# Windowed attention and a low-rank mixer on one core: load order, shared Q/K buffers and new places for three batches' attention

## The chip, the core and the metric

The kernel runs on one core of one Trainium2 chip. The core has five engines that run side by side, each through its own list of instructions in order: TensorE (PE, matrix products; PEld are its weight loads), VectorE (DVE), ScalarE (ACT), GpSimd (POOL) and SyncE (SP). POOL and SP here also issue the DMAs that bring data from HBM to the on-chip memory SBUF and back. Matrix products land in a small accumulator memory, PSUM, from which DVE and ACT read. An instruction waits on semaphores that other engines and DMAs count up.

The metric is the device time of one execution in microseconds; several runs of the kernel are made, and their median is given.

## What is computed

Inputs are q, k and v of shape (8 batches, 8 heads, 576 positions, 64), the low-rank factors U (576 x 32) and V (32 x 576), and two weight matrices w_ch1 (512 x 2048) and w_ch2 (2048 x 512). In short form:

```python
scores = (q @ k.transpose(0, 1, 3, 2)) / 8          # per batch and head
scores = where(0 <= row - column < 64, scores, -1e9)  # a causal window of 64
attn = softmax(scores) ; a = attn @ v
x = a.transpose(0, 2, 1, 3).reshape(8, 576, 512)
h = x.transpose(0, 2, 1) @ U @ V                     # mixes positions, rank 32
u = x + h.transpose(0, 2, 1)
out = u + maximum(u @ w_ch1, 0) @ w_ch2              # per position
```

Results are float32; the kernel works in bfloat16 with float32 accumulation.

## The kernel before

The 8 x 576 = 4608 positions are also 9 chunks of 512. The two big products over w_ch1 and w_ch2 run chunk by chunk (function `mlp`, L635 to L680): 16 pieces `ch1`, each four matmuls of 512 columns and a relu on ACT or DVE, and 16 pieces `ch2` of four matmuls each, whose every fourth adds u on DVE (`osb`) and sends 128 rows out through SP. These 32 pieces, and an empty one behind them, are the slots 0 to 32 of a chunk.

The attention of a batch is cut into small pieces (function `attention`, L238 to L629), and each piece is hung behind a slot of the chunk before the one that needs it. Batch 0 is worked off at the start, batch c + 1 within chunk c. The tables `PLACE`, `PLACE_0`, `PLACE_1` and `PLACE_2` (L683 to L711) give the slot for each piece: T or TX turns K and Q, S multiplies them and takes the exponential on ACT, M multiplies with the window mask on DVE, PV multiplies with V and divides by the row sums on DVE, U and V are the two low-rank products, and UT turns the result u into the layout that `ch1` reads. Nothing reorders this: `tc.manual_schedule()` keeps each engine's instructions in the order in which the program emits them. The frame around it adds the waits: an instruction that reads a buffer waits for the last one that wrote it in program order, and one that writes waits for earlier readers.

Batches 0 and 1 are loaded in a grouped layout, 96 partitions with 6 positions each (tiles `kg` and `qg` of a pool of four, L104 to L121), and turned on PE into `kf` and `qf` (pieces `TK` and `TQ`, L270 to L280); ACT copies K out of PSUM, and DVE copies Q. From batch 2 on K and Q arrive in a natural layout, 128 positions at a time, in `kn` and `qn` (two buffers each, L91), and SP turns them by DMA (`TX`, L282 on). There is one `kf` and one `qf`. V arrives in `vA`; a copy shifted by 64 positions, `vB`, is made by `shift_v` (L146 to L152): on POOL for batches 0 and 1, on DVE from batch 2 on.

POOL issues all loads in this order: K and Q of batch 0, V of batch 0, the two halves of w_ch1 (`w1b`), copies for batch 0's `vB`, K and Q of batch 1, V of batch 1, four quarters of w_ch2 (`w2b`, L225), copies for batch 1's `vB`, then at the head of each chunk's emission (L783 to L796) K and Q of batch 2 (chunk 0 only), V of batch c + 2, and K and Q of batch c + 3. The pieces of chunk c are emitted after these loads, in the loop that fills the slots (L811 on).

PSUM has eight banks: `ps_big` holds two double ones (scores, PV results, the low-rank products), `ps_tp` one (turned tiles), and from chunk 0 on `mm` has three for `ch1` and `ch2`. Batches 0 to 2 turn u on PE with an ACT copy behind (`UT`, L589 to L602); from batch 3 (`NXU = 3`) SP does it by DMA.

At the start the mask is built on POOL and DVE (`maskA`, ones and zeros; `maskB`, zeros and -30000, which PE adds to batch 0's scores), and PE runs idle products (`turn_over`, L716) between pieces.

The softmax here doesn't subtract the row's maximum and nothing guards it: scores larger than these inputs give would overflow.

## Time and profile before

| | |
|---|---|
| median of 3 runs | 322.46 us (321.39 to 322.79) |
| the profiled execution's own time | 320.92 us |
| its span, first to last instruction | 319.2 us |
| PE busy | 304.6 us |
| DVE, ACT, POOL busy | 163.1, 101.8, 103.2 us |
| data moved by DMA | 39.56 MB |
| mean granted PE clock | 0.999 |

The profile is one execution, taken by the hardware. Its times count from the first instruction. "Busy" is the time in which an engine works on something of its own; issuing and waiting are not in it, except that POOL's DMA issues, for which it writes descriptors, are. The list of groups gives for each source line, engine and operation the tiles (output<-inputs), the shape, the count, the busy time and the mean of one in nanoseconds, and then the engine's idle time just before them with what ended most of it. The list of waits says who waited for whom: total in us, times, longest. The order in time gives start, length, engine, line and operation, equal neighbours merged. A matmul of 512 columns is listed with some 380 ns, but neighbours overlap: 64 of them in a row take 13.81 us, so 0.216 us each, and a slot of four 0.86 us.

Chunk 0 begins at 23.69 us, its `ch2` pieces at 43.20, chunk 1 at 64.51, chunk 2 at 98.31 and chunk 3 at 131.66 us. From there on a chunk with attention takes some 32.1 us and one without 27.6.

### The profile page before, as it was taken

Reading aid. Unit: us, or ns where it says so; the run is one execution under the profiler, and the core shown is the slowest. Engines: PE = TensorE matmul, PEld = TensorE weight load, DVE = VectorE, ACT = ScalarE, POOL = GpSimd, SP = SyncE. Lnnn points to the kernel's source line nnn. Section 1 sums busy time; section 2 is a strip of 40 time slices with the busy share of each in tenths; the row PEclk is TensorE's granted clock in tenths of the full one; section 3 lists DMA queues with packets and bytes.
Section 4 is the critical chain, followed back from the end, with each engine's and each line's share of the span. In section 5 each row is a group of like instructions: output and inputs, shape, how many; then the busy total and the mean of one; then the engine's idle time right before and its main releaser. Section 6 shows DMA issues by size and latency. Waiting matters only on the chain.

```text
span 319.2 us, 6811 instructions
## 1 busy us (share of the span) xinstructions
PE 304.6 (95%) x2829; PEld 148.9 (47%) x2855; DVE 163.1 (51%) x293; ACT 101.8 (32%) x160; POOL 103.2 (32%) x134
## 2 busy tenths in 40 slices
PE   6879988999999999899999999999999999999995
PEld 6544543544454544354445444544454444444442
DVE  4464584537675854475647454756474443016011
ACT  2645550337124440345033502350245003201500
POOL 8591696645744744555543400000000000000000
PEclk9999999999999999999999999999999999999999
DMA  7999999999999999999999994444200520020011
GB/s 103 165 225 202 153 201 171 114 185 179 148 124 218 157 127 138 193 179 156 146 204 167 138 162 150 68 100 103 98 2 2 115 100 2 11 87 33 2 66 66
DMA packets 151871, 39.56 MB, mean 124 GB/s; under 512 B 140960, under 2 KB 146080, under 8 KB 151840
## 3 DMA queue, kind: packets, MB, share of 16 engines
q0 software_dynamic: 100096, 18.36, 82.2%
q1 hardware_dynamic: 51744, 20.77, 37.0%
q8 instruction: 22, 0.36, 0.5%
q14 instruction: 9, 0.07, 0.1%
HBM read 37.14 MB, written 9.44 MB: 146 GB/s over the span
## 4 chain that ended last, share of the span: by engine, by line
PE 80%; DMA 13%; POOL 5%; issue 1%; DVE 0%; POOLq 0%
PE psU L665 36%; PE psA L643 35%; DMA qg<-in_q_dram 5%; DMA vA<-in_v_dram 3%; DMA uTc<-un 3%; PE psv L566 2%; DMA qn<-in_q_dram 2%; PE sc L326 2%; PE xw L388 2%; POOL vB L149 1%; POOL vB L152 1%; PE xr L388 1%; PE pshh L487 1%; PE tpu L598 1%; POOL kg L117 1%
## 5 line engine op out<-in xcount | busy, mean ns | idle before, releaser
L665 PE MATMUL psU<-w2b,c 128*128 128x512 bf16 x555 | 130.3, 379 | 3.6 <-DMA w2b<-in_moe_w_ch_dram 2.3
L643 PE MATMUL psA<-uTc,w1b 128*128 128x512 bf16 x576 | 131.0, 380 | 1.6 <-DMA uTc<-un 1.1
L665 PEld LDWEIGHTS <-c 128*128 128x128 bf16 x576 | 55.2, 98 | 66.8 <-issue 3.0
L643 PEld LDWEIGHTS <-w1b 128*128 128x128 bf16 x576 | 54.0, 98 | 66.3 <-DMA uTc<-un 1.6
L654 ACT ACTIVATE c<-psA 128x512 bf16<-128x512 f32 x83 | 49.6, 597 | 91.3 <-PE psA L643 91.2
L674 DVE TENSOR_TENSOR osb<-psU,un 128x512 f32<-128x512 f32 x36 | 24.9, 691 | 82.9 <-PE psU L665 82.7
L652 DVE TENSOR_SCALAR c<-psA 128x512 bf16<-128x512 f32 x61 | 42.1, 690 | 25.8 <-PE psA L643 25.8
L579 DVE TENSOR_TENSOR un<-psv,xs 128x512 bf16<-128x512 f32 (+1 forms) x40 | 25.4, 683 | 22.1 <-PE psv L566 22.0
L135 POOL DMA_DIRECT2D vA<-in_v_dram x32 | 28.1, 888 | 19.8 <-DMA kn<-in_k_dram 6.4
L126 POOL DMA_DIRECT2D qn<-in_q_dram x30 | 25.3, 843 | 22.9 <-DMA vA<-in_v_dram 12.8
L346 ACT ACTIVATE pts<-sc 128x1024 bf16<-128x1024 f32 x32 | 31.4, 1028 | 2.3 <-PE sc L326 2.2
L126 POOL DMA_DIRECT2D kn<-in_k_dram x30 | 25.8, 859 | 15.9 <-DMA vA<-in_v_dram 9.4
L379 ACT ACTIVATE ptl<-low 128x256 bf16<-128x256 f32 x5 | 1.9, 384 | 65.8 <-PE high L326 65.8
L352 DVE TENSOR_TENSOR pts<-pts,maskA 128x1024 bf16<-128x1024 bf16 x28 | 19.1, 682 | 0.1
L326 PEld LDWEIGHTS <-kf 64*64 64x64 bf16 x704 | 9.9, 107 | 8.2 <-issue 8.0
L326 PE MATMUL sc<-qf,kf 64*64 64x128 bf16 (+1 forms) x624 | 12.1, 212 | 1.2 <-issue 0.4
L388 PEld LDWEIGHTS <-pts 128*64 128x64 bf16 x512 | 10.2, 110 | 6.1 <-issue 3.7
L566 PE MATMUL psv<-hh,vrep 128*128 128x512 bf16 x40 | 12.5, 379 | 0.0
L455 DVE TENSOR_TENSOR xs<-xw,rcw 128x896 bf16<-128x896 f32 x10 | 10.9, 1092 | 0.3
L411 DVE TENSOR_TENSOR xs<-xr,rcp 128x512 bf16<-128x512 f32 (+1 forms) x15 | 10.4, 690 | 0.5
L502 ACT CAST hh<-pshh 128x512 bf16<-128x512 f32 x7 | 4.1, 581 | 16.9 <-PE pshh L495 16.9
L601 ACT COPY uTc<-tpu 128x512 bf16<-128x512 bf16 x9 | 5.3, 586 | 11.2 <-PE tpu L598 11.2
(102 smaller groups left out, 159.7 us busy)
## 6 DMA issues: line engine op xcount, KB each, us to landing
out_dram<-osb SPq DMA_DIRECT2D x36, 256.0 KB, 2.4
vA<-in_v_dram POOLq DMA_DIRECT2D x32, 128.0 KB, 10.9
kn<-in_k_dram POOLq DMA_DIRECT2D x24, 128.0 KB, 12.5
qn<-in_q_dram POOLq DMA_DIRECT2D x24, 128.0 KB, 12.1
w1b<-in_moe_w_ch_dram POOLq DMA_DIRECT2D x2, 1024.0 KB, 16.3
w2b<-in_moe_w_ch_dram POOLq DMA_DIRECT2D x4, 512.0 KB, 12.8
kg<-in_k_dram POOLq DMA_DIRECT2D x2, 288.0 KB, 5.8
qg<-in_q_dram POOLq DMA_DIRECT2D x2, 288.0 KB, 6.6
```

The costliest lines, as they stand in the source:

```text
L126: nc.gpsimd.dma_start(out=dst[0:rows, t, :, :], in_=src[b, :, t * P : t * P + rows, :].rearrange("h p d -> p h d"),)
L135: nc.gpsimd.dma_start(out=va[:, t, :, 0:D], in_=v[b, :, t * P : (t + 1) * P, :].rearrange("h p d -> p h d"),)
L326: nc.tensor.matmul(sc[g][r0 : r0 + W, col * W : (col + n) * W], keys_of(j, u, rs), queries_of(j, blk, n, rs), start=not spare, stop=last o ...
L346: nc.scalar.activation(out=dst, in_=sc[:], func=ACT.Exp, scale=scale)
L352: nc.vector.tensor_tensor(out=dst, in0=dst, in1=maskA.rearrange("p g n w -> p g (n w)"), op=ALU.mult)
L388: nc.tensor.matmul(dst, pts[:, h // 2, h % 2, blk, :] if blk < NB - 1 else ptl[:, h // 2, h % 2, :], rhs, start=True, stop=True,)
L579: nc.vector.tensor_tensor(out=u_tiles[g][rs, :], in0=ps[0][rs, n, :], in1=x[rs, t, :, :].rearrange("p h d -> p (h d)"), op=ALU.add,)
L643: nc.tensor.matmul(ps[:], w1b[:, dc, i * P : (i + 1) * P], uTc[:, :, dc, :], start=(dc == 0), stop=(dc == NDC - 1),)
L652: nc.vector.tensor_relu(out=c1[i][:], in_=ps[:])
L654: nc.scalar.activation(out=c1[i][:], in_=ps[:], func=ACT.Relu)
L665: nc.tensor.matmul(acc[t][:], c1[i][:, t * P : (t + 1) * P], w2b[:, i, :], start=(i == 0), stop=(i == NFC - 1),)
L674: nc.vector.tensor_tensor(out=osb[:], in0=acc[t][:], in1=u_tiles[g][:], op=ALU.add)
```

## The change

Seven things change together.

1. **Load order.** The four quarters of w_ch2 are issued before V of batch 1.
2. **Shifted V.** For batch 0 two of the seven copies move from POOL to ACT. Batch 1's copies move from POOL to DVE, as pieces `SV` in slots 21 to 24 of chunk 0, ahead of the PV pieces that read them.
3. **Q/K buffers.** The pool of four grouped tiles goes. Two buffers each, `kr` and `qr`, hold K and Q of batches b and b + 2 in turn: the grouped layout in their first 96 partitions for batches 0 and 1, the natural one from batch 2 on. The calls that issue loads stand where they stood. `kf` and `qf` are doubled.
4. **Places.** The pieces of batches 1 to 3 move: `PLACE_1` and `PLACE_2` change, `PLACE_3` is new, and a place of 100 + s means slot s of the next chunk. Batch 3 turns u on PE (`NXT = 4`).
5. **Mask.** The repeated columns of `maskB` are copied by ACT and DVE; those of `maskA` are made by DVE after batch 0's last piece.
6. **First slots.** In chunk 0 the first two `ch1` pieces run interleaved; which engine takes which relu changes in chunks 0 to 2.
7. **Small ones.** Batch 0's fourth Q copy goes from ACT to DVE, and one more idle product follows the third mask product.

```diff
     NXU = 3
+    NXT = 4
     GP = S // GR
...
     vB = [const.tile([P, NFULL, H, VW], BF16, name=f"vB{i}") for i in range(2)]
-    kn = [const.tile([P, NT, H, D], BF16, name=f"kn{i}") for i in range(2)]
-    qn = [const.tile([P, NT, H, D], BF16, name=f"qn{i}") for i in range(2)]
-    kf = const.tile([P, NT * HP * P], BF16, name="kf")
-    qf = const.tile([P, NT * HP * P], BF16, name="qf")
-    kt, qt = ([f[:, j * S : (j + 1) * S] for j in range(HP)] for f in (kf, qf))
-    kx, qx = (f.rearrange("p (t j w) -> p t j w", t=NT, j=HP) for f in (kf, qf))
+    kr = [const.tile([P, H * GR * D], BF16, name=f"kr{i}") for i in range(2)]
+    qr = [const.tile([P, H * GR * D], BF16, name=f"qr{i}") for i in range(2)]
+    kn, qn = (
+        [r[:, 0 : NT * DM].rearrange("p (t h d) -> p t h d", t=NT, h=H) for r in rs] for rs in (kr, qr)
+    )
+    kfs = [const.tile([P, NT * HP * P], BF16, name=f"kf{i}") for i in range(2)]
+    qfs = [const.tile([P, NT * HP * P], BF16, name=f"qf{i}") for i in range(2)]
     pts = const.tile([P, HP, 2, NB - 1, W], BF16, name="pts")
...
         if grouped:
-            kb = kg_pool.tile([GP, H, GR, D], BF16, name="kg")
-            qb = kg_pool.tile([GP, H, GR, D], BF16, name="qg")
+            kb, qb = (
+                r[0:GP, :].rearrange("p (h c d) -> p h c d", h=H, c=GR) for r in (kr[b % 2], qr[b % 2])
+            )
         else:
...
         if grouped:
-            step = 4 if split else H
-            for h0 in range(0, H, step):
-                hs = slice(h0, h0 + step)
+            for h0, h1 in ((0, 4), (4, 8)) if split else ((0, H),):
+                hs = slice(h0, h1)
                 for t, src in ((kb, k), (qb, q)):
...
             copy(out=vb[0:W, lo:last, :, :], in_=va[0:W, lo + 1 : last + 1, :, :])
+    def shift_high(b, copy, t):
+        copy(out=vB[b % 2][W:P, t, :, :], in_=vA[b % 2][W:P, t, :, :])
+    def shift_low(b, copy, t):
+        copy(out=vB[b % 2][0:W, t, :, :], in_=vA[b % 2][0:W, t + 1, :, :])
...
     for i in range(2):
-        nc.vector.memset(kn[i][W:P, NFULL, :, :], 0.0)
-        nc.vector.memset(qn[i][W:P, NFULL, :, :], 0.0)
+        nc.vector.memset(kn[i][GP:P, NFULL, :, :], 0.0)
+        nc.vector.memset(qn[i][GP:P, NFULL, :, :], 0.0)
...
         nc.gpsimd.dma_start(out=w1b[:, :, lo:hi], in_=w1v[:, :, lo:hi])
-    for t in range(NFULL):
-        shift_v(0, nc.gpsimd.tensor_copy, range(t, t + 1))
+    for t in range(2):
+        shift_high(0, nc.gpsimd.tensor_copy, t)
+        shift_low(0, nc.gpsimd.tensor_copy, t)
+    shift_low(0, nc.gpsimd.tensor_copy, 2)
     for _ in load_kq(1, False):
         pass
-    load_v(1)
     w2v = moe_w_ch2.rearrange("(i p) m -> p i m", p=P)
...
         nc.gpsimd.dma_start(out=w2b[:, i : i + 4, :], in_=w2v[:, i : i + 4, :])
-    for t in range(NFULL):
-        shift_v(1, nc.gpsimd.tensor_copy, range(t, t + 1))
+    load_v(1)
...
         pcs = {}
+        kf, qf = kfs[odd], qfs[odd]
+        kt, qt = ([f[:, j * S : (j + 1) * S] for j in range(HP)] for f in (kf, qf))
+        kx, qx = (f.rearrange("p (t j w) -> p t j w", t=NT, j=HP) for f in (kf, qf))
...
             def f():
-                copy = nc.scalar.copy if spare and j == 3 else nc.vector.tensor_copy
-                copy(out=place_of(qt, j), in_=tr(qb, j, b == 1))
+                nc.vector.tensor_copy(out=place_of(qt, j), in_=tr(qb, j, b == 1))
             return f
...
                 dst = uT_of(g // TPC)[:, g % TPC, :, :]
-                if b >= NXU:
+                if b >= NXT:
                     nc.sync.dma_start_transpose(out=dst, in_=u_tiles[g][:])
...
-    DVE_RELU = {0: (8, 10, 11, 13, 15), 1: (2, 4, 6, 9, 10, 12, 13)}
+    DVE_RELU = {0: (7, 9, 11, 15), 1: (2, 4, 6, 8, 10, 12, 15), 2: (1, 3, 6, 7, 9, 10)}
     DVE_RELU_N = (0, 1, 2, 4, 5, 6, 8)
...
-        def ch1(i):
-            def f():
-                ps = psum["mm"].tile([P, CH], FP32, name="psA", tag="mm")
+        def ch1(*ids):
+            def f():
+                ps = {i: psum["mm"].tile([P, CH], FP32, name="psA", tag="mm") for i in ids}
                 for dc in range(NDC):
-                    nc.tensor.matmul(
-                        ps[:],
-                        w1b[:, dc, i * P : (i + 1) * P],
-                        uTc[:, :, dc, :],
-                        start=(dc == 0),
-                        stop=(dc == NDC - 1),
-                    )
-                c1[i] = c1_pool.tile([P, CH], BF16, name=f"c1_{i}")
-                if i in DVE_RELU.get(c, DVE_RELU_N):
-                    nc.vector.tensor_relu(out=c1[i][:], in_=ps[:])
-                else:
-                    nc.scalar.activation(out=c1[i][:], in_=ps[:], func=ACT.Relu)
+                    for i in ids:
+                        nc.tensor.matmul(
+                            ps[i][:],
+                            w1b[:, dc, i * P : (i + 1) * P],
+                            uTc[:, :, dc, :],
+                            start=(dc == 0),
+                            stop=(dc == NDC - 1),
+                        )
+                for i in ids:
+                    c1[i] = c1_pool.tile([P, CH], BF16, name=f"c1_{i}")
+                    if i in DVE_RELU.get(c, DVE_RELU_N):
+                        nc.vector.tensor_relu(out=c1[i][:], in_=ps[i][:])
+                    else:
+                        nc.scalar.activation(out=c1[i][:], in_=ps[i][:], func=ACT.Relu)
             return f
...
-        return [ch1(i) for i in range(NFC)] + [ch2(t, r) for t in range(TPC) for r in range(4)]
+        ups = [ch1(i) for i in range(NFC)]
+        if c == 0:
+            ups[0:2] = [ch1(0, 1), lambda: None]
+        return ups + [ch2(t, r) for t in range(TPC) for r in range(4)]
...
     PLACE_1 = {
-        "T": [11, 11, 12, 12, 13, 13, 14, 14],
-        "S": [12, 13, 14, 15, 15],
-        "M": [13, 14, 15, 16, 16],
-        "PV": [17, 17, 18, 19, 20],
-        "U": [22],
-        "V": [23, 24, 25],
-        "UT": [25, 26, 27, 28, 29],
-        "TX": [20, 22, 24, 26, 28],
+        "T": [10, 10, 11, 11, 12, 12, 13, 13],
+        "S": [11, 12, 13, 14, 15],
+        "M": [12, 13, 14, 15, 16],
+        "SV": [21, 22, 23, 24],
+        "PV": [21, 22, 23, 24, 24],
+        "U": [26],
+        "V": [27, 28, 28],
+        "UT": [29, 30, 31, 31, 102],
+        "TX": [27, 28, 29, 30, 31],
     }
     PLACE_2 = {
-        "S": [8, 8, 11, 11, 13],
-        "M": [9, 10, 12, 13, 14],
-        "PV": [16, 16, 18, 18, 20],
-        "TX": [13, 14, 15, 16, 17],
-        "U": [21],
-        "V": [23, 24, 25],
-        "UT": [25, 26, 27, 28, 29],
+        "S": [14, 14, 17, 17, 18],
+        "M": [15, 16, 18, 19, 19],
+        "PV": [20, 20, 22, 22, 24],
+        "TX": [20, 21, 22, 23, 24],
+        "U": [26],
+        "V": [27, 28, 29],
+        "UT": [29, 30, 31, 102],
+    }
+    PLACE_3 = {
+        "S": [5, 5, 5, 8, 8],
+        "M": [5, 6, 7, 9, 10],
+        "PV": [12],
+        "TX": [12, 13, 14, 15, 16],
+        "U": [18],
+        "V": [20, 21, 22],
+        "UT": [22, 23, 24, 25, 102],
     }
...
     )
-    pair = maskA[:, 0, 1:3, :].rearrange("p (o n) w -> p o (n w)", o=1)
-    nc.vector.tensor_copy(
-        out=maskA[:, 0, 3:7, :].rearrange("p (o n) w -> p o (n w)", o=2),
-        in_=pair.to_broadcast([P, 2, 2 * W]),
-    )
-    nc.vector.tensor_copy(out=maskA[:, 0, 7, :], in_=maskA[:, 0, 1, :])
     nc.vector.tensor_scalar(
-        out=maskB[:],
-        in0=maskA[:, 0, :, :],
+        out=maskB[:, 0:3, :],
+        in0=maskA[:, 0, 0:3, :],
         scalar1=30000.0,
...
     )
+    def repeat(copy, mask):
+        pair = mask[:, 1:3, :].rearrange("p (o n) w -> p o (n w)", o=1)
+        copy(
+            out=mask[:, 3:7, :].rearrange("p (o n) w -> p o (n w)", o=2),
+            in_=pair.to_broadcast([P, 2, 2 * W]),
+        )
+        nc.vector.tensor_copy(out=mask[:, 7, :], in_=mask[:, 1, :])
+    repeat(nc.scalar.copy, maskB)
     order = "K0 K1 B0 B1 Q0 Q1 S0 S1 K2 K3 B2 Q2 B3 Q3 S2 S3 B4 S4"
...
             load_low_rank()
-        turn_over({"B1": 1, "Q1": 1, "S1": 1, "Q3": 1}.get(what, 0))
-    nc.vector.tensor_copy(out=maskA[:, 1, :, :], in_=maskA[:, 0, :, :])
+        turn_over({"B1": 1, "Q1": 1, "S1": 1, "B2": 1, "Q3": 1}.get(what, 0))
     nc.scalar.copy(out=ub[0][:], in_=uf[0][:])
+    for t in range(2, NFULL):
+        shift_high(0, nc.scalar.copy, t)
     nc.scalar.copy(out=vrep[:, W : W + S], in_=vf[:])
...
         f()
+    repeat(nc.vector.tensor_copy, maskA[:, 0])
+    nc.vector.tensor_copy(out=maskA[:, 1, :, :], in_=maskA[:, 0, :, :])
     first.close()
...
+    all_slots = [[[] for _ in range(NSLOT + 1)] for _ in range(NCH)]
     for c in range(NCH):
-        slots = [[] for _ in range(NSLOT + 1)]
+        slots = all_slots[c]
...
                 for f, s in zip(att[b][part], where[part]):
-                    slots[s].append(f)
+                    all_slots[c + s // 100][s % 100].append(f)
...
                     pass
-            where = {1: PLACE_1, 2: PLACE_2}.get(b, PLACE)
+            where = {1: PLACE_1, 2: PLACE_2, 3: PLACE_3}.get(b, PLACE)
             if b < NXB:
...
                     )
+            if b == 1:
+                def land(t):
+                    def f():
+                        shift_high(1, nc.vector.tensor_copy, t)
+                        if t > 0:
+                            shift_low(1, nc.vector.tensor_copy, t - 1)
+                    return f
+                att[1]["SV"] = [land(t) for t in range(NFULL)]
+                place(b, ("SV",), where)
             place(b, ("S", "M", "PV"), where)
```

More of the change, by code (lines that the diff above doesn't have):

```diff
@@ L59 @@
     const = ctx.enter_context(tc.tile_pool(name="const", bufs=1))
-    kg_pool = ctx.enter_context(tc.tile_pool(name="kg", bufs=4))
     uT_pool = ctx.enter_context(tc.tile_pool(name="uT", bufs=3))
```

## The prediction

> **What bounds the kernel now.** I read the page's engine line and the chain that ended last, then the list of waits of PE, then the order of POOL and PE in time between 28 and 52 us.
>
> ```profile
> PE 304.6 (95%) x2829; PEld 148.9 (47%) x2855; DVE 163.1 (51%) x293; ACT 101.8 (32%) x160; POOL 103.2 (32%) x134
> ```
>
> ```profile
> PE psU L665 <- DMA w2b<-in_moe_w_ch_dram: 2.3, 3, 1.1
> ...
> PE psA L643 <- DMA uTc<-un: 1.1, 1, 1.1
> ```
>
> The span is 319.2 us, and PE is busy for 304.6 of it. A gain can only come from the 14.6 us in which PE is idle. Of these some 6 lie before 24 us and 3.7 after the last matmul; between stand the two waits of the list, 2.3 us for the second weights in chunk 0 and 1.1 us for a transposed batch at the start of chunk 3. A new PE wait lengthens the run at once, because PE has no slack that could take it up.
>
> POOL issues the loads one behind the other (columns: start, length, what; in brackets the idle time before and what ended it):
>
> ```profile
> 28.95 0.76 POOL L225 DMA_DIRECT2D w2b<-in_moe_w_ch_dram  x1 [4.08 <-DMA w1b<-in_moe_w_ch_dram]
> 31.89 0.74 POOL L225 DMA_DIRECT2D w2b<-in_moe_w_ch_dram  x1 [2.18 <-DMA kg<-in_k_dram]
> 35.43 1.50 POOL L225 DMA_DIRECT2D w2b<-in_moe_w_ch_dram  x2 [2.80 <-DMA qg<-in_q_dram]
> ```
>
> An issue waits until the load eight places ahead of it has landed; so batch 1's Q landed at about 35.2 us. PE took it up at once:
>
> ```profile
> 35.23 0.45 PE L262 MATMUL tpg<-ident,kg 96*64 96x96 bf16 x12
> 35.51 0.42 PE L262 MATMUL tpw<-ident,qg 96*64 96x96 bf16 x12
> 35.87 1.04 PE L643 MATMUL psA<-uTc,w1b 128*128 128x512 bf16 x4
> 36.84 0.45 PE L262 MATMUL tpg<-ident,kg 96*64 96x96 bf16 x12
> ```
>
> How fast the one queue of loads runs is read from the GB/s at the end of three stretches: the second weights (39 to 46), V (36 to 38), and K and Q in natural layout (48.5 to 52):
>
> ```profile
> 36.00:38.00 2.00, 2.00 (x47) 1.16 (x46) 1.16 (x3) 1.42 (x4) 1.92 (x4) 1.00 2.23 133
> 39.00:46.00 7.00, 6.62 (x155) 3.75 (x151) 5.52 (x9) 5.14 (x7) 6.82 (x9) 1.00 1.25 205
> 48.50:52.00 3.50, 2.32 (x27) 1.02 (x30) 2.17 (x5) 0.00 (x0) 1.96 (x3) 1.00 2.39 154
> ```
>
> **Part 1: the shared K/Q buffers.** The changed kernel drops the pool of grouped tiles. Batch 1's grouped K and Q now lie in kr1 and qr1, which are also the natural buffers of batch 3. At the head of chunk 0 the program issues the loads of batch 2, V of 2, and K and Q of batch 3; the pieces of batch 1's transposes are emitted later, from slot 10 on. In program order a reader follows the last writer before it, and the order of the instructions with their waits shows just that: the first K transpose of batch 1 waits for batch 3's first two K loads, the first Q transpose for the first two Q loads, the third pair for all ten. (So batch 1's scores are made from batch 3's rows.) In the kernel before, other tiles held them and the wait was for kg and qg alone. Behind the waiting transpose on PE stands all that is left; ACT, DVE and SP run dry.
>
> When do those loads land? From 35.2 on the queue has to move, in the new order: four second-weight loads at 512 KB, 2.10 MB at 205 GB/s = 10.2 us; V of batch 1, 0.59 MB at 133 = 4.4; K and Q of batch 2, 1.18 MB at 154 = 7.7; V of batch 2, 4.4; then four of batch 3's loads, 0.52 MB at 154 = 3.4. Sum 30.1: the second Q load lands at 65.3, and the tenth 4.3 us later, at 69.6. Nothing on PE, DVE or SP holds these issues up: the buffers' former readers are batch 0's, done by 22 us.
>
> Without the wait PE would do the first pair one slot earlier than before, at 35.23 - 0.86 = 34.37, and end the third Q at 34.37 + 1.61 + 1.95 + 0.64 = 38.57 (a pair to the next is 1.61 without and 1.95 with a score piece, by the rows at 35.23, 36.84 and 38.79). With the wait it starts the first Q at 65.3 and has 3.6 us of work before the third Q, which is at the earliest 69.6; it ends by 70.0. That is **+31.4**.
>
> Bounds: had all bytes moved at 205 GB/s, the tenth load would land at 62.7, 6.9 us less; in the kernel before, the V issue at 77.08 ended a wait of 1.48 for batch 3's third load, which this sum has at 64.5, so 12.6 more, beside transposes of batch 2 on SP. I take the middle rows, because SP's transposes now stand behind an output of slot 27 that PE has not reached.
>
> PE stands still for 31 us and starts cold. The warm-up at the start shows the price (96-column matmuls, from 1.25 us and from 4.51 us):
>
> ```profile
> 1.25 2.18 PE L718 MATMUL unread<-idle 128*128 128x96 bf16 x25 [1.25 <-DVE idle L156]
> ...
> 4.51 0.81 PE L718 MATMUL unread<-idle 128*128 128x96 bf16 x15
> ```
>
> 25 starts by 3.2 us are 78 ns each, 15 in the last 0.63 us of it are 42: half speed for the first 3.3 us. Of the 3.6 us of work 1.65 is done by 68.6, the rest by 70.5, so the third Q starts 0.9 later than its load allows: **+0.9**, between 0 (no slow start) and 3.4 (two such stretches). The Trainium skill's "TensorE: Matmul & The Clock Gate" (Part 1) says that an idle window of about 3.4 us halves the clock, and that a busy one restores it; by its full penalty of 1.7 the sum would be 0.8 more. The first stretch is seen here, a fall after a pause in mid-run in no row.
>
> **Part 2: the second weights first.** They land at 45 us, PE comes to them after 70: **-2.3**, all of the first wait.
>
> **Part 3: batch 1 placed anew.** The copies of V into its shifted twin move from POOL to DVE, two for each PV piece, in slots 21 to 24. On DVE they stand behind the reciprocal and the product of the PV piece before, and the next PV waits for them.
>
> ```profile
> L411 DVE TENSOR_TENSOR xs<-xr,rcp 128x512 bf16<-128x512 f32 x12 | 8.3, 691 | 0.4
> ...
> L152 DVE COPY vB<-vA 64x1560 bf16<-64x1560 bf16 x6 | 4.0, 669 | 0.1
> ...
> L410 DVE RECIPROCAL rcp<-xr 128x8 f32<-128x8 f32 x12 | 2.4, 203 | 6.3 <-PE xr L388 6.3
> ...
> L758 DVE COPY maskA<-maskA 128x512 bf16<-128x512 bf16 x1 | 0.3, 282 | 0.0
> ```
>
> The path from one PV to the next is 0.2 from PE to DVE + 0.21 + 0.69 + two copies + 0.13 back. No row shows a 64x520 copy on DVE; between 0.28 (L758) and 0.67 (L152, three times its size) I take 0.4, for the smaller size is nearer. That is 2.03, less 0.16 by which neighbours on DVE overlap; one slot of matmuls (0.86) covers part, so 1.0 is left, three times, and once an osb of 0.69 stands between: **+3.6**, from 2.9 to 5.2 by the ends of the copy. The Trainium skill's "SBUF — State Buffer" (Who interferes with whom) holds that a two-port DVE copy and GpSimd block each other whole. L735, 256 columns in 0.67 us while POOL wrote descriptors, against 0.28 for 512 columns agrees; were all six copies so caught, the term would be 5.2, and 2.9 by L758's row.
>
> Two V pieces in slot 28 want a third score buffer where there are two; the second waits for two additions of 0.68 behind an osb: **+0.5** (0 to 0.8). The last two transposes of batch 1 stand after the chunk's last matmul, with one PSUM tile between them:
>
> ```profile
> L601 ACT COPY uTc<-tpu 128x512 bf16<-128x512 bf16 x9 | 5.3, 586 | 11.2 <-PE tpu L598 11.2
> ```
>
> Each costs 0.04 + 0.59 + 0.13 in which PE has nothing: **+1.5** (1.3 to 2.0). Before, five such copies lay under matmuls, at slots 25 to 29.
>
> **Part 4: batches 2 and 3.** At the end of chunk 1 one copy of that kind is bare: **+0.75**. In slot 19 an osb goes ahead of the last mask products: **+0.5**; in slot 24 the shift of the next V (0.78 + 0.67) goes ahead of the last product that U waits for: **+0.5** (both 0 to 1.2). Batch 3's five result transposes move from SP to PE: five times 0.22 = **+1.1**, and chunk 3's wait goes: **-1.1**. The double transposed buffers free SP's transposes from the scores before them; these gave PE no wait in the list: 0. Covered by 20 us from slot 27 of chunk 0 to slot 14 of chunk 1, batch 2's later transposes (10 issues of some 1.4 in SP's rows from 51.97, and up to the page's 7.8 to land) are about in time: cost 0, up to 2 if they take all of it.
>
> **Part 5: start.** The mask on two engines (0.67 + 0.55 + 0.29 on DVE before, then a part on ACT) ends before 6.6, when the first K lands; one more warm-up matmul is 0.2 us ahead of a wait of 0.47 for the first chunk; the paired first matmuls add none. 0, between -0.3 and +0.3, for the load of the first weights ends the start in both.
>
> **Sum.** 31.4 + 0.9 - 2.3 + 3.6 + 0.5 + 1.5 + 0.75 + 0.5 + 0.5 + 1.1 - 1.1 = +37.4 on the profiled execution's 320.9 us: 358.3. The median of the runs shown is 1.5 above that execution, so a median of the changed kernel may lie between 358.3 and 359.8; I say 359.
>
> **Rivals.** (a) The queue runs as it did beside SP's transposes: every load 12.6 later, sum 371. For it: 12 us of such traffic in the rows from 62 on. Against it: SP is held behind PE here. (b) The queue runs at the weights' rate throughout, the clock does not fall and the DVE terms are at their low ends: 358.3 - 6.9 - 0.9 - 0.7 - 0.5 - 1.0 = 348. Against it: 154 GB/s for K in two separate stretches. (c) The other side: batch 1's transposes do not wait for batch 3's loads. Place: the first K of slot 10; price -32.3. With the placement terms (7.35) it leaves 326.0, and faster than before only if these stay under 2.3, for then the weights' wait gained outweighs them: 318.6 at nothing. It is decided by whether the second Q load of batch 3 has landed by some 37 us; the first weights' two halves alone keep the queue to about 29. (d) The move of weights does nothing by itself: true in part, for its 2.3 are swallowed by the larger wait; the sum is unchanged.
>
> **How the numbers follow.** My case (350 to 367) 0.77, (a) 0.09, (b) 0.11, (c) 0.03. Range 348 to 369, which holds the case, most of (b) and the lower part of (a). Within 0.5% is about what this kernel's measurement cannot tell from no change. Faster 0.02, same 0.01, slower 0.97, the first two from (c).
>
> **What would show it.** Right: a PE wait of about 31 us at the first K or Q transpose of batch 1, put down to a load of kr or qr; smaller ones at the third pair; no wait for w2b; PV waits on vB copies of near 1 us in chunk 0; an ACT copy as what ends the idle time before chunks 1 and 2. Wrong: no wait at slot 10, or batch 3's second Q load before 60 or after 72 us.

## The result and the profile after

The changed kernel takes 356.87 us (median of 4 runs, 356.31 to 357.49); the kernel before took 322.50 in the same comparison (321.39 to 322.79). The ratio is 1.107, with a 95% interval of 1.104 to 1.111. The profiled execution took 357.49 us, with a span of 355.8. Medians and ranges, here and below, are over all executions; ratios leave out those that lie over 1.5% above the fastest of their kernel.

The page's line of engines, and of its forty slices those of PE and of PE's granted clock (8.9 us a slice, busy share and clock in tenths):

```profile
PE 313.0 (88%) x2876; PEld 152.0 (43%) x2876; DVE 163.9 (46%) x300; ACT 106.5 (30%) x169; POOL 97.3 (27%) x125
...
PE   7898000897989999999999999999999999999995
...
PEclk9999655599999999999999999999999999999999
```

PE was busy for 95% of the span before and is for 88% now. Smaller gaps that went and came aside, the difference is one hole between 34 and 62 us, with the clock at half until nearly 70 us. The list of waits of PE (total in us, times, longest) names what ends it:

```profile
PE tpg L272 <- DMA kr<-in_k_dram: 29.9, 3, 28.2
PE xr L397 <- DVE vB L159: 2.2, 3, 1.3
PE psA L653 <- ACT uTc L610: 1.3, 2, 0.7
...
PE tpu L607 <- ACT uTc L610: 0.7, 1, 0.7
...
PE psv L575 <- DVE un L588: 0.5, 1, 0.5
```

The 2.3 us for the second weights and the 1.1 for `uTc` at chunk 3 are gone. In their place stands a wait of 29.9 us for K loads into `kr`, and four smaller ones that the prediction names. In PE's order in time the first row is batch 1's first K transpose:

```profile
62.42 0.42 PE L272 MATMUL tpg<-ident,kr 96*64 96x96 bf16 x5 [28.22 <-DMA kr<-in_k_dram]
63.84 0.53 PE L272 MATMUL tpg<-ident,kr 96*64 96x96 bf16 x7 [1.01 <-DMA kr<-in_k_dram]
64.10 1.11 PE L272 MATMUL tpw<-ident,qr 96*64 96x96 bf16 x12
65.14 1.89 PE L653 MATMUL psA<-uTc,w1b 128*128 128x512 bf16 x4
...
70.14 0.45 PE L272 MATMUL tpg<-ident,kr 96*64 96x96 bf16 x12
70.42 0.42 PE L272 MATMUL tpw<-ident,qr 96*64 96x96 bf16 x12
```

The load that ends the wait is not batch 1's. Batch 1's K and Q landed at 31.3 and 34.2 us. Those that landed at 62.28 and 63.80, just ahead of the rows at 62.42 and 63.84, are batch 3's first two K loads, issued from 57.23 on. They overwrite batch 1's rows before the transposes read them, so the changed kernel makes batch 1's scores from batch 3's K and Q, which is not what the function asks for. POOL's order in time shows where they stand in the queue:

```profile
19.55 3.01 POOL L233 DMA_DIRECT2D w2b<-in_moe_w_ch_dram  x4
23.94 0.98 POOL L136 DMA_DIRECT2D vA<-in_v_dram  x1 [1.38 <-DVE uTc L562]
...
40.29 0.89 POOL L127 DMA_DIRECT2D kr<-in_k_dram  x1 [2.32 <-DMA w2b<-in_moe_w_ch_dram]
...
53.09 3.55 POOL L136 DMA_DIRECT2D vA<-in_v_dram  x4
...
57.23 0.96 POOL L127 DMA_DIRECT2D kr<-in_k_dram  x1
```

So the queue works off the second weights, V of batch 1, K and Q of batch 2, V of batch 2, and only then what PE stands waiting for. The moments at which each group had landed, beside the prediction's working:

| last of | predicted | landed |
|---|---|---|
| second weights | 45.4 | 44.39 |
| V of batch 1 | 49.8 | 50.05 |
| K, Q of batch 2 | 57.5 | 57.20 |
| V of batch 2 | 61.9 | 62.10 |
| batch 3's second Q load | 65.3 | 64.64 |
| batch 3's tenth load | 69.6 | 68.87 |
| third Q transpose's end | 70.9 (69.6 + 0.4 + 0.9) | 70.84 |

Here is the granted clock in four stretches (columns: stretch; length and PE busy, with the matmuls; clock; busy share of the DMA engines; GB/s):

```profile
36.00:40.00 4.00, 0.00 (x0) 0.88 1.24 206
40.00:62.00 22.00, 0.00 (x0) 0.50 2.42 141
62.00:70.00 8.00, 6.43 (x74) 0.51 1.72 111
70.00:74.00 4.00, 4.00 (x93) 1.00 0.01 2
```

PE has work again from 62.42 on but stays at half clock until 69.77; the four matmuls at 65.14 take 1.89 us where four at full clock take 1.04.

### The profile page after: what moved, and what is told of

Its sections match the earlier page's. It is cut to its first block, busy times and chain, and to the rows that moved or that the text cites. A ratio compares the mean times of both kernels' runs of the same rounds, so it can differ in the third digit from the quotient of the medians.

```text
span 355.8 us, 6890 instructions
## 1 busy us (share of the span) xinstructions
PE 313.0 (88%) x2876; PEld 152.0 (43%) x2876; DVE 163.9 (46%) x300; ACT 106.5 (30%) x169; POOL 97.3 (27%) x125
## 4 chain that ended last, share of the span: by engine, by line
PE 76%; DMA 12%; POOL 4%; DVE 4%; issue 2%; ACT 1%; POOLq 0%; DVEq 0%
PE psA L653 34%; PE psU L676 33%; DMA vA<-in_v_dram 5%; DMA w1b<-in_moe_w_ch_dram 5%; PE sc L335 2%; PE psv L575 2%; POOL vA L136 1%; PE xw L397 1%; DMA qr<-in_q_dram 1%; DVE xs L420 1%; DVE osb L685 1%; PE tpu L607 1%; PE xr L397 1%; POOL kr L127 1%; PE pshh L496 1%
## 5 line engine op out<-in xcount | busy, mean ns | idle before, releaser
L653 PE MATMUL psA<-uTc,w1b 128*128 128x512 bf16 x576 | 132.5, 382 | 1.8 <-ACT uTc L610 1.3
L676 PE MATMUL psU<-w2b,c 128*128 128x512 bf16 x576 | 132.1, 379 | 0.0
L665 ACT ACTIVATE c<-psA 128x512 bf16<-128x512 f32 x85 | 50.6, 597 | 92.7 <-PE psA L653 92.7
L663 DVE TENSOR_SCALAR c<-psA 128x512 bf16<-128x512 f32 x59 | 40.6, 689 | 32.0 <-PE psA L653 32.0
L355 ACT ACTIVATE pts<-sc 128x1024 bf16<-128x1024 f32 x32 | 31.4, 1030 | 5.4 <-PE sc L335 5.4
L127 POOL DMA_DIRECT2D kr<-in_k_dram x30 | 26.4, 879 | 20.0 <-DMA kf<-kr 14.4
L272 PE MATMUL tpg<-ident,kr 96*64 96x96 bf16 x60 | 3.0, 238 | 29.9 <-DMA kr<-in_k_dram 29.9
L127 POOL DMA_DIRECT2D qr<-in_q_dram x30 | 26.7, 892 | 7.5 <-DMA qf<-qr 3.9
L288 DVE COPY qf<-tpw 128x576 bf16<-128x576 bf16 x4 | 3.0, 757 | 34.1 <-PE tpw L272 34.1
L272 PEld LDWEIGHTS <-kr 96*64 96x64 bf16 x96 | 2.9, 121 | 32.8 <-DMA vA<-in_v_dram 28.7
L610 ACT COPY uTc<-tpu 128x512 bf16<-128x512 bf16 x14 | 8.2, 585 | 16.2 <-PE tpu L607 16.2
```

The lines of the kernel that those rows point to most:

```text
L127: nc.gpsimd.dma_start(out=dst[0:rows, t, :, :], in_=src[b, :, t * P : t * P + rows, :].rearrange("h p d -> p h d"),)
L355: nc.scalar.activation(out=dst, in_=sc[:], func=ACT.Exp, scale=scale)
L653: nc.tensor.matmul(ps[i][:], w1b[:, dc, i * P : (i + 1) * P], uTc[:, :, dc, :], start=(dc == 0), stop=(dc == NDC - 1),)
L663: nc.vector.tensor_relu(out=c1[i][:], in_=ps[i][:])
L665: nc.scalar.activation(out=c1[i][:], in_=ps[i][:], func=ACT.Relu)
L676: nc.tensor.matmul(acc[t][:], c1[i][:, t * P : (t + 1) * P], w2b[:, i, :], start=(i == 0), stop=(i == NFC - 1),)
```

## The experiments

They ask three things: what makes the wait (the first four), what the other parts cost once it is gone, and whether a version without it beats the kernel before. Over all these runs the kernel before had medians of 321.9 to 322.1.

### Batch 3's loads issued behind batch 1's transposes

```diff
-            if b + 2 < B:
+            if b + 2 < B and b > 1:
                 for _ in load_kq(b + 2, False):
                     pass
...
                 place(b, ("T",), where)
+                slots[13].append(lambda: [None for _ in load_kq(3, False)])
```

> The changed kernel, with one thing moved: batch 3's K and Q loads are issued behind batch 1's transposes (slot 13 of chunk 0) instead of at the head of chunk 0. Loads, bytes, buffers and places stay. Theory A (PE waits because batch 1's transposes follow batch 3's loads into the shared buffers): the third Q transpose ends near 38.6 instead of 70.8 us, the wait on kr of 29.9 us falls to under 0.5, no slow clock in mid-run; 356.9 - 32.2 = 324.7, taken as 324 to 326. The PV, psv and UT waits (2.2 + 0.5 + 2.0) stay. Rival B (the new order of the queue and the moved placement cost the time, the shared buffers do not): PE keeps a wait of over 20 us in chunk 0, time above 340.

Measured: 327.49 us (ratio to before 1.016, 1.011 to 1.020). The 34.4 us of loss shrink to 5.4: theory A, and B falls. With the loads behind them, the transposes also read batch 1's own rows again. The third Q transpose ends at 38.61 us; the prediction's sum without a wait had 38.57. But the time is 1.5 above the top of what A allowed. PE's waits and the clock in chunk 0 show why:

```profile
PE xr L397 <- DVE vB L159: 2.9, 3, 1.6
...
PE tpg L272 <- DMA kr<-in_k_dram: 0.6, 1, 0.6
```

```profile
52.00:54.00 2.00, 0.39 (x11) 1.00 2.33 161
54.00:56.00 2.00, 1.41 (x20) 1.00 2.00 214
56.00:58.00 2.00, 1.44 (x33) 0.59 2.29 171
58.00:60.00 2.00, 2.00 (x7) 0.56 2.83 147
```

Two things are new. The PV waits on the V copies are 2.9 instead of 2.2 us, with longer copies while POOL issues loads beside them: in this half of chunk 0 it is busy for 22.4 of 25.9 us, in the changed kernel for 6.0 of 23.6. The same DVE copies, first in the changed kernel, then here (count, busy time, mean in ns):

```profile
L156 DVE COPY vB<-vA 64x520 bf16<-64x520 bf16 x4 | 1.2, 291 | 0.1
L159 DVE COPY vB<-vA 64x520 bf16<-64x520 bf16 x3 | 0.9, 288 | 0.0
```

```profile
L156 DVE COPY vB<-vA 64x520 bf16<-64x520 bf16 x4 | 1.6, 394 | 0.1
L159 DVE COPY vB<-vA 64x520 bf16<-64x520 bf16 x3 | 1.1, 378 | 0.0
```

Three of the seven copies took 0.35, 0.64 and 0.56 us here, the other four 0.29 as before. That POOL's issues are the reason fits these rows, but no run tests it by itself.

And PE idled so much between 52.9 and 56.3 us that its clock fell to half from 56.34 to 59.76, which costs half of 3.4 us. 0.7 and 1.7 on 324.7 make 327.1.

### Batch 3's K and Q ahead of batch 2's V

```diff
-            if b + 1 < B:
+            if b + 1 < B and b > 1:
                 load_v(b + 1)
             if b + 2 < B:
                 for _ in load_kq(b + 2, False):
                     pass
+            if b == 1:
+                load_v(b + 1)
```

> The changed kernel, with V of batch 2 issued behind batch 3's K and Q instead of ahead of them; batch 1's scores are made from batch 3's rows, as in the changed kernel. Theory A (the wait ends when batch 3's tenth K/Q load lands, and the queue works its list in order): every one of these loads lands 4.9 us earlier, which is what V of batch 2 took (57.2 to 62.1); the wait on kr falls from 29.9 to about 25, time 356.9 - 4.9 = 352.0 (351.3 to 352.7). Rival (PE waits for the whole of what was issued at the head of the chunk, or for something else in the queue): 356.9, no change.

Measured: 352.67 us, 4.2 less by the medians; 4.79 less between the two profiled executions (352.70 and 357.49), and the third Q transpose ends 4.79 earlier (66.05). The wait is as A had it:

```profile
PE tpg L272 <- DMA kr<-in_k_dram: 24.9, 3, 23.5
```

The wait ends when its own loads land, and what the queue carries ahead of them counts one for one.

### Idle products inside the wait

```diff
+                def keep_busy():
+                    ps = ps_tp.tile([P, CH], FP32, name="busy", tag="tp")
+                    for _ in range(125):
+                        nc.tensor.matmul(ps[:], idle[:, 0:P], idle[:], start=True, stop=True)
+
+                slots[10].append(keep_busy)
```

> The changed kernel, with 125 idle products of 512 columns (27 us at 0.216 each) on PE just before batch 1's first K transpose, inside the wait; batch 1's scores are made from batch 3's rows, as in the changed kernel. Theory A (after the wait PE works at half clock until about 4.9 us later, and this costs time): granted clock 1.0 from about 36 us on, the wait on kr falls from 29.9 to some 3, the third Q transpose ends 0.4 behind the tenth load (68.87) at 69.3 instead of 70.8; time lower by 0.9 (the prediction's term) to 1.5, 355.4 to 356.0. Rival B (the slow clock costs nothing, the loads alone set the end): 356.9. Rival C (the wait is not idle time, the added products lengthen the run): up to 384.

Measured: 356.07 us (354.84 to 357.35), 0.8 under the changed kernel's median, with ranges that overlap; the medians alone do not decide between A and B. C falls: 27 us of added work cost nothing. The profile decides for A:

```profile
40.00:60.00 20.00, 19.89 (x93) 1.00 2.36 149
60.00:66.00 6.00, 5.45 (x56) 1.00 2.47 144
```

With the clock kept up, the third Q transpose ends at 69.10, 0.40 behind the tenth load (68.70); in the changed kernel 1.97 behind it (70.84 and 68.87). The slow clock costs 1.57 us. From that transpose to the end of the span both need 284.9 us.

### The shared buffers alone

The kernel before with the parts of the change that replace `kg`, `qg`, `kn` and `qn` by `kr` and `qr`, and nothing else.

> The kernel before, with one part of the change alone: K and Q of batches b and b + 2 share two buffers each (kr, qr). Load order, places, one kf and one qf, the mask and POOL's copies of V stay as before. Batch 1's scores are made from batch 3's rows. Theory A (the sharing and the order of the calls make the wait, whatever else is moved): PE waits some 30 us in slots 11 to 14 of chunk 0 on kr and qr, the w2b wait of 2.3 goes, nothing else changes; 322.5 + 32.2 - 2.3 = 352, taken as 349 to 357. Rival B (sharing alone is harmless, the wait needs the new load order or the new places): 322 to 324.

Measured: 348.30 us (347.72 to 349.74), 26.3 above before.

```profile
PE tpg L265 <- DMA kr<-in_k_dram: 28.1, 3, 25.8
```

Theory A, and B falls: sharing alone makes the wait, with the old load order and the old places. The number is 3.7 below the one expected, and 0.7 under its range, as the expectation took the shift of the changed kernel. Here the transposes stand one slot later, so the third Q moves from 39.49 to 70.72, by 31.2 only; the weights' wait of 2.3 goes, and the wait at chunk 3, which I had left out, goes too (chunk 2 lasts 32.1 instead of 33.4). 31.2 - 2.3 - 1.3 = 27.6, and the span grew by 27.4.

### The second weights first, alone

```diff
-    load_v(1)
     w2v = moe_w_ch2.rearrange("(i p) m -> p i m", p=P)
     for i in range(0, NFC, 4):
         nc.gpsimd.dma_start(out=w2b[:, i : i + 4, :], in_=w2v[:, i : i + 4, :])
+    load_v(1)
```

> The kernel before, with one part of the change alone: the four quarters of the second weights are issued ahead of batch 1's V; batch 1's shifted copies stay on POOL and its PV pieces in slots 17 to 20. Theory A (the two loads share one queue, so what the weights gain V loses): the w2b wait of 2.6 (as PE's gaps) goes, V's tiles land at 45.4 to 49.3 instead of before 42, POOL's copies of 0.62 each follow them, and PV in slots 17 to 20 waits some 3.5 to 4 us in sum; time 322 to 325. Rival B (the early weights are a plain gain): 319.5 to 320.

Measured: 327.93 us, with a wide spread (323.66 to 329.53); ratio 1.012 (1.004 to 1.019). The list of PE's waits in the profiled execution (323.66):

```profile
PE sc L326 <- DMA qf<-qn: 2.1, 1, 2.1
PE tpu L598 <- DVE un L579: 2.0, 1, 2.0
PE xr L388 <- POOL vB L152: 1.5, 1, 1.5
```

B falls: the move is no gain by itself. A is right in kind and wrong in place. PV waits for 1.8 us in all (1.5 and 0.36 for V), not 3.5 to 4, and two waits of 2 us turn up in chunk 1, at batch 2's scores and result transposes: POOL, held by the copies, issued batch 2's first K load at 50.7 instead of 42.0, and V of batch 3 landed at 96.0 instead of 90.9. The median lies above A's 322 to 325, the profiled execution within it; what made the other three executions 3.6 to 5.9 us longer is not shown.

### Copies on ACT, and earlier places

Both start from the kernel with late loads. The first puts batch 1's V copies on ACT:

```diff
-                        shift_high(1, nc.vector.tensor_copy, t)
+                        shift_high(1, nc.scalar.copy, t)
                         if t > 0:
-                            shift_low(1, nc.vector.tensor_copy, t - 1)
+                            shift_low(1, nc.scalar.copy, t - 1)
```

> The kernel with the late loads (batch 3's K and Q behind batch 1's transposes; 327.5 us), and batch 1's seven shifted copies of V on ACT (0.62 each, as in the rows of batch 0) instead of DVE. Theory A (there the copies on DVE, of which three took 0.35 to 0.64 instead of 0.29 while POOL wrote descriptors, make the 2.9 of PV waits, and these gaps bring the half clock of 56.34 to 59.76, worth 1.7): waits on vB under 0.5, granted clock 1.0 all through chunk 0, 327.5 - 2.6 - 1.7 = 323.2 (322.4 to 324). Rival B (V's landing at 45.4 to 49.3 holds PV, whoever copies): the waits stay, 327. Rival C (the waits go but the clock falls all the same): 325.

The second also moves batch 1's pieces up, and batch 2's last PV and transposes:

```diff
-        "SV": [21, 22, 23, 24],
-        "PV": [21, 22, 23, 24, 24],
-        "U": [26],
-        "V": [27, 28, 28],
-        "UT": [29, 30, 31, 31, 102],
+        "SV": [19, 20, 21, 22],
+        "PV": [20, 21, 22, 23, 23],
+        "U": [25],
+        "V": [26, 27, 28],
+        "UT": [27, 28, 29, 30, 102],
```

> As the kernel with late loads and copies on ACT, and batch 1's PV to UT pieces one slot or so earlier (PV 20 to 23, U 25, V 26 27 28, UT 27 to 30), batch 2's last three result transposes in slots 28 to 30. Theory A (the bare result transposes and the third score buffer cost what their gaps show, 0.67 three times and 0.5): all four gaps go, 323.2 - 2.5 = 320.7 (319.8 to 321.6), a little under the kernel before. Rival B (the work behind them is only pushed on, PV then waits for V's landing instead): 322.5 to 323.5.

Measured: 327.87 (325.49 to 330.29) and 329.09 us (327.85 to 330.18). Neither is faster than the 327.49 they start from, though each gained what it was meant to: the waits on `vB`, then those on `uTc` and `psv`, are gone, and chunk 1 starts at 64.6 and 61.7 us instead of 69.3. None of the rivals named what takes it back. Most of it is given back in chunk 2, at batch 3's scores; first the row of the one, then of the other, and the other's clock there:

```profile
PE low L335 <- DMA qf<-qr: 4.4, 1, 4.4
```

```profile
PE low L335 <- DMA qf<-qr: 4.5, 1, 4.5
```

```profile
107.00:111.00 4.00, 0.57 (x33) 0.68 1.39 169
111.00:115.00 4.00, 4.00 (x39) 0.50 1.53 190
```

PE waits for SP's transposes of batch 3's Q, then runs at half clock for 6.8 us, 3.4 us of work lost. The second kernel loses more in chunk 1: 2.6 us of waiting for batch 2's `qf`, and 1.7 by a half clock from 77.72 to 81.13. (Both profiled executions are the longest of their kernels.) `PLACE_2` of the change has these ten transposes in slots 20 to 24 of chunk 1, where before they stood in 13 to 17. In the changed kernel this costs nothing, since chunk 2 begins at 134.5.

### Batch 3's, then batch 2's transposes in their old slots

The kernel with the earlier places, and batch 3's transposes moved back:

```diff
     PLACE_2 = {
...
-        "TX": [20, 21, 22, 23, 24],
+        "TX": [13, 14, 15, 16, 17],
```

> The kernel with late loads, copies on ACT and earlier pieces (329.1 us), with SP's transposes of batch 3's K and Q placed in slots 13 to 17 of chunk 1, as before the change, instead of 20 to 24. Theory A (the change's place for these ten transposes makes the 4.5 us that PE waits for batch 3's scores in chunk 2, and the half clock of 108.44 to 115.26 behind it, worth 3.4; in the changed kernel itself both lie hidden, since chunk 2 begins 30 us later): 329.1 - 7.9 = 321.2 (320 to 323). Rival B (the transposes are paced by the loads of K and Q, not by their place): 327 to 329.

Measured: 322.40 us (320.93 to 323.78), ratio to before 1.000 (0.997 to 1.003). Theory A; the wait in chunk 2 and the slow clock are both gone. With its loads, copies and places mended in this way, the change is now level with the kernel before. One wait of 1.7 for batch 2's `qf` remains in chunk 1; the next run moves batch 2's transposes too:

```diff
     PLACE_1 = {
...
-        "TX": [27, 28, 29, 30, 31],
+        "TX": [20, 22, 24, 26, 28],
```

> The kernel with batch 3's transposes in slots 13 to 17 of chunk 1 (322.4 us), batch 2's transposes on SP in slots 20, 22, 24, 26, 28 of chunk 0, as before the change, instead of 27 to 31. Theory A (their late place makes the 1.7 that PE waits on qf in chunk 1): that wait goes, 320.7 (320 to 321.5). Rival B (the transposes end when the DMA engines let them, in either place): 322 to 323.

Measured: 325.43 us (322.92 to 327.24). The wait for `qf` goes, as A had it, and the time rises by 3.0, which neither theory had. A list of the waits of PE, and one of DVE from 85 to 98 us:

```profile
PE tpu L607 <- DVE un L588: 4.1, 1, 4.1
```

```profile
DVE vB L150 <- DMA vA<-in_v_dram: 5.5, 1, 5.5
```

With batch 2's transposes 8 to 9 us earlier the loads come later: V of batch 3 lands from 86.3 to 94.9 instead of 80.4 to 88.8 us. DVE stands at its copy in slot 24 of chunk 1, and behind that copy stand the additions that batch 2's result transposes want. Behind PE's wait the clock is at half from 96.70 to 100.11, which costs another 1.7. So 4.1 and 1.7 come and the 1.7 for `qf` goes; the profiled span grew by 4.0.

### A version from the other end

The kernel before with few moves: second weights first, batch 1's copies on ACT and its places as in the kernel above, batch 3's U, V and UT one slot up.

```diff
-    load_v(1)
     w2v = moe_w_ch2.rearrange("(i p) m -> p i m", p=P)
...
-    for t in range(NFULL):
-        shift_v(1, nc.gpsimd.tensor_copy, range(t, t + 1))
+    load_v(1)
...
+    PLACE_3 = dict(PLACE, U=[13], V=[15, 16, 17], UT=[16, 16, 17, 17, 18])
```

> The kernel before with only these: second weights ahead of batch 1's V; batch 1's shifted copies on ACT in slots 19 to 22, its PV in 20 to 23, U 25, V 26 27 28, UT 27 to 30 and slot 2 of chunk 1; batch 3's U, V and UT one slot earlier. Own Q/K buffers, one kf and one qf, the mask and batch 2's places stay. Theory A (the two PE waits of the kernel before are all that can be had): the w2b gaps of 2.6 go, 0.9 of the 1.1 at the start of chunk 3 goes, up to 0.5 is given back at PV: 322.3 - 3.2 = 319.1 (318.3 to 320). Rival B (V behind the weights comes too late for PV in slots 20 to 23): 321 to 323.

Measured: 320.74 us (318.21 to 324.02), ratio 0.995 (0.992 to 0.999), between the two theories. Most of the 3.2 us is given back at the same DVE copy; first PE's wait, then DVE in order of time:

```profile
PE tpu L596 <- DVE un L577: 3.1, 1, 3.1
```

```profile
93.25 0.70 DVE L149 COPY vB<-vA 64x2080 bf16<-64x2080 bf16 x1 [3.98 <-DMA vA<-in_v_dram]
93.98 0.81 DVE L152 COPY vB<-vA 64x1560 bf16<-64x1560 bf16 x1
94.72 1.87 DVE L577 TENSOR_TENSOR un<-psv,xs 128x512 bf16<-128x512 f32 x3
```

In the kernel before this copy started at 91.55, and the tile that it reads last had landed at 90.85: there were 0.7 us of slack, so a larger gain ahead of it had to meet V of batch 3. But the landing moved as well: here DVE was ready for the copy at 89.28, 2.2 us earlier than before, and that tile landed at 93.06, 2.2 us later. Why it came later no run shows. The next two take that copy out of chunk 1 and put batch 3's result transposes on PE:

```diff
+    NXT = 4
...
-                if b >= NXU:
+                if b >= NXT:
...
-    PLACE_3 = dict(PLACE, U=[13], V=[15, 16, 17], UT=[16, 16, 17, 17, 18])
+    PLACE_3 = dict(PLACE, S=[1, 1, 1, 3, 3], M=[1, 2, 3, 4, 5], UT=[19, 20, 21, 22, 23])
...
-                    slots[slot].append(
+                    (slots[slot] if bs != 3 else all_slots[2][6]).append(
```

> The kernel of the four small moves (320.7 us), with batch 3's shifted V copies moved from slot 24 of chunk 1 to slot 6 of chunk 2, batch 3's scores one slot later, and its five result transposes on PE instead of SP. Theory A (the 3.1 us that PE waited in chunk 1 came from DVE, which stood behind V of batch 3 until 93.1 with the result additions queued behind it): that wait goes, the 0.5 at the start of chunk 3 goes, 1.1 of PE work comes: 320.7 - 2.5 = 318.2 (317.3 to 319). Rival B (the loads and SP's transposes are what holds PE until some 130 us; an earlier PE meets them at the next place, batch 3's scores or chunk 3): 320 to 321.5.

Measured: 320.93 us (319.93 to 324.37), not under the one before, and in rival B's range. The two waits are gone, but PV of batch 3 waits 1.2 for the copy in its new place. In this profiled execution the clock also fell in the start (18.07 to 21.48), and chunk 0 began 1.3 us later than in the one before it.

```diff
-                    (slots[slot] if bs != 3 else all_slots[2][6]).append(
+                    (slots[slot] if bs != 3 else all_slots[2][3]).append(
```

> The kernel with batch 3's V copies moved to chunk 2 (320.9 us), these copies in slot 3 instead of slot 6. Theory A (in slot 6 they end 0.9 before PV of batch 3 wants them, behind two relus and two mask products on DVE, and cost the 1.15 that PE waits on vB): that wait goes, 319.8 (319 to 320.6). Rival B (DVE has too much in the first slots of chunk 2, the wait goes to the mask products or a relu): 320.9 or more.

Measured: 319.53 us (318.69 to 325.04), ratio to before 0.993 (0.990 to 0.996). Theory A, and it beats both kernels, the one before by 0.7%. The largest of PE's waits left are all of the start:

```profile
PE unread L719 <- DVE idle L157: 1.3, 1, 1.3
PE xr L387 <- DVE rcp L409: 0.6, 1, 0.6
PE tpg L261 <- DMA kg<-in_k_dram: 0.6, 1, 0.6
```

## Why the prediction was right, point by point

**The wait of part 1 (+31.4, and +0.9).** Right in place, cause and size. The third Q ends at 70.84; against 38.57 that is 32.3, the two terms' sum. Late loads take the wait away, an earlier place in the queue shortens it by what it skips, and the buffers alone bring it. That the size fits so well is in part luck, for errors cancel. The last loads came 0.7 earlier than worked out, and that is itself a balance: batch 1's Q landed at 34.23 and not at 35.2, its V took 5.7 us and not 4.4, and batch 3's first four loads took 2.5 and not 3.4. The slow clock was mis-sized: 1.57 instead of 0.9. The term had half clock for 3.3 us from the first work on; it lasted 7.3. PE's first products came in pieces between waits (the row at 63.84), and the clock stayed at half through them. The sign named ahead, one wait of about 31 us, came as 28.2, since PE took up batch 3's first K loads one by one as they landed.

**The weights' wait (-2.3).** Gone, and the order alone is no gain (rival d, as it was priced): its gain goes to other waits. Some expectations count 2.6 for it; two gaps of 0.16 in that figure stand where the list holds a slot's weight loads but lacks one of its matmuls, and are no waits.

**Part 3.** PV waits: 3.6 said, 2.2 found (0.42, 1.26, 0.55). Two steps of the term were off. The copy was taken at 0.4 and took 0.29, the low end. And the cover between two PV pieces is 1.12, not 0.86: behind a PV that ended at 86.10 the slot's matmuls and the next piece's first product, on `vA`, ran until 87.22, and the release came at 87.77. The third score buffer: 0.5 said, 0.51 found. Result transposes at the end of chunk 0: 1.5 said, 1.35 found. The price by which POOL hinders the copies was in the working as an upper end; it fits that the copies are slower only where POOL has loads to issue (291 against 394 ns above).

**Part 4.** The bare transpose at the end of chunk 1: 0.67, said 0.75. Mask products: 0.21, said 0.5. The last product before U: 0.07, said 0.5. Batch 2's later transposes at 0, with 20 us of cover: right in the changed kernel. The text named that cover but not what the other ten transposes, batch 3's, cost without it: 4.4 us and a slow clock, as soon as chunk 2 begins at 100 instead of 134.5.

**Sum.** These gaps make 32.3 - 2.3 + 2.2 + 0.5 + 1.35 + 0.95 + 1.1 - 1.1 = 35.0, where the prediction had 37.4; PE's last matmul moved by 36.3 (315.46 to 351.74). So 1.3 that no term held made up for half of what the terms had too much. Some 0.6 of it lies in chunk 0's second half, which grew by 2.3 us where its gaps grew by 1.8; what makes it no run tested. The forecast for the median was 359, and 356.87 was measured: the profiled execution, at 357.49, is 0.8 under the sum's 358.3, and the median lies 0.6 below that execution, where 0 to 1.5 above it was assumed.

**The rivals.** (a), a slower queue, had SP's transposes beside the loads for its reason; SP started them at 92.9, long after the wait. (b), all bytes at the weights' rate, fails on the table of landings. (c), no wait, was priced at 326.0 with the placement terms; the run without the wait gave 327.49, and the surplus of 1.5 is about what the slow clock behind the PV gaps costs (1.7). The remark that it would gain only with placement terms under 2.3 fits: there the PV waits alone were 2.9, and it lost. The limit itself was not tested.

**Open.** Batch 3's transposes, the V copies and the loads were each moved, but not the DMA engines' load itself: how far transposes and loads slow each other for the same bytes was not measured apart.

## What to carry to other kernels

When two users take turns in one buffer, it is the order of emission that says what a reader waits for: a load that is hoisted ahead of the reader of the old contents becomes what that reader waits for, and the contents are lost with it. After removing a PE wait, look for the next wait in line (here a DVE copy with 0.7 us of slack and ten transposes on SP) before booking the gain: three moves that were each right gave nothing until those were placed too. And a new wait is dearer than its length where it drags the clock down behind it.

## What the runs showed of the hardware

The clock went down and up in steps. In all the traces its slow stretches, but for the start and the last moments of a run, last 3.41 us or a whole multiple: 3.41 (late loads; some kernels at 18 us), 6.83 (the ACT copies), 27.3 (batch 3's loads first), 30.7 (the changed kernel). Laid out in windows of that length, without the first of each run and those of its last 10 us, PE's idle time in one goes with the clock in the next: 18 windows at full clock with 1.0 to 1.5 us idle were followed by full clock; of eight with 1.5 to 1.9 idle four were, four were not; of seven with over 1.9 none was. (One with 1.91 in the last 10 us of a run was; idle time is known to some 0.2 us, since the lists lack a few matmuls.) A window with 1.05 idle (62.9 to 66.4 in the changed kernel) did not bring a half clock back to full. So a gap of 3.1 us split between two windows cost no clock (the version with few moves), and one of 1.6 with smaller ones around it did (late loads). The Trainium skill's "TensorE: Matmul & The Clock Gate" (Part 1) gives a free-running window of 3413 ns, and the durations agree; it speaks of an idle window, and here 1.6 to 1.9 us idle in one were sometimes enough. The spread of some kernels here may come from where the windows fall: of the executions of the kernel with the ACT copies the shortest (325.49 us) had a mean granted clock of 1.000 and the longest (330.29) one of 0.988. That was not tested.
